# Sixteen sign pairs, swapped-part products and a new instruction order in a two-headed sequence kernel

## The chip, the cores and the metric

The kernel runs on one core of one Trainium2 chip. The metric is the device time of one execution in microseconds (us). Three runs of the kernel before gave 344.28, 345.22 and 346.68 us; their median is 345.22 us. One more execution was taken with the hardware profiler; its trace is the source of every duration below.

## The reference

Two independent results are computed for a sequence of 2048 positions and 448 channels, and joined along the channels.

```python
def _A_ref(x, wqkv, w_phi, wo):              # linear attention, 16 heads of 28
    q, k, v = (x @ wqkv), split into heads
    phi_q = concat(softmax(q @ w_phi), softmax(-(q @ w_phi)))     # phi_k likewise
    kv = einsum("bhsf,bhsd->bhfd", phi_k, v);  z = sum of phi_k over s
    o = (phi_q @ kv) / (phi_q . z + 1e-6)
    return o @ wo
def _B_ref(u, A, B, C, log_dt, Dskip):       # state-space convolution, 256 states a channel
    l = arange(2048) in bfloat16
    K = einsum("dn,dnl,dn->dl", C, exp(dt * A * l), dt * B).real
    return causal convolution of u with K (by FFT of length 4096) + u * Dskip
```

Because `l` is rounded to bfloat16, K has only 641 different positions.

## The kernel before

**The attention half.** A preparation folds `w_phi` into the key and query weights and transposes x. `key_side` then walks over 16 blocks of 128 positions: TensorE makes the key and value products (L577), ScalarE takes the exponentials with both signs (L580) and copies the values (L582), VectorE sums, inverts and scales (L584, L588, L590), TensorE accumulates (L594). `query_side` runs four times, on 512 positions each (q0 to q3): TensorE makes the query products (L610), ScalarE takes 8 exponentials (L613), TensorE makes the denominators (L619), VectorE divides (L626 to L631) and scales (L641), TensorE transposes and projects (L648, L654) and ScalarE copies (L650, L656).

**The convolution half.** The channels are worked through in four quarters `qt`, each in two chunks `c` of 112 columns. For every quarter there are two tables of complex powers. `U` has 16 high rows and is built by `hi_tables` on VectorE, doubling the rows with the powers 32, 64, 128 and 256 (`table_cmul`, L521 to L524, four operations for each product). `W` has 48 low rows at the positions `LO`: 15 pairs +p and -p, the rows 0 and 16 by themselves, and 16 far rows at 512, 1024 and 1536 plus something. `rotations(qt)` fills `T` with sines and cosines on ScalarE (L485, L486); `dampings(qt)` writes exponentials into `W` on ScalarE (L499, L502) and a negated copy (L503). Then `damp(qt, c)` on VectorE multiplies `W` by `T` (L535 on 15 rows of one part, L537 on one row) and makes the far rows from near ones with the conjugate of the power 512 (three `table_cmul`). `build_k` contracts both tables over the states on TensorE (L564) and ScalarE copies the result (L568). `scatter_k` moves it by DMA into `Kt`. `kernel_spectrum` (L697, copies L700), the spectrum of u (`signal_spectrum`, sums and differences at L305 and L306, products L317, copies L320) and `conv_group` (products L713, sums L718 to L760, `inverse` L725 to L729, TensorE L738) make the convolution in a transformed domain; the results are copied at L745 and stored.

**What sets the order.** `in_order` reads a table `ORDER` with one entry each for TensorE (PE), ScalarE (ACT), VectorE (DVE) and the DMA queue of SyncE (SP), and ties every engine to the order that it lists. No instruction can overtake another on its engine. The preparation, the key side, the four query parts and the four quarters are interleaved in this order. Most tables live in one large SBUF tile at byte offsets written in the code, so that buffers share space (for instance the ring `LATE` of late constants, `EQ` of the query exponentials, and the key weights `WpK` and `WV`).

ScalarE holds one set of function tables at a time; an `ACT_TABLE_LOAD` row stands wherever the order goes from exponentials to sines or back. Copies and casts stand between both without a load.

Of the kernel before, what the change touches and what calls it, by code (L numbers as in the profile page):

```python
# [36 lines left out]
LO = [s * p for p in LO_ABS[:-1] for s in (1, -1)] + [0, 16]  # L37
# [57 lines left out]
def pair_rows(x2, row, t, col):  # L95
# [11 lines left out]
        '8{^3b6Y5Jf$Tog2C_YVvp0dKPh9Q4@xt{w8^JtU(*2MZ52W>;7_d`){S@B+R9&}>lv1dU0dK5ovINDB67xgl9iN6qtG(uIee=B9)ok3m'
        'grrhuGFx$M%8cN}G^?%OE?~|Xhp7OiMdG9Fh{ZdLlHgvfkjbOIVzXJD=`yq~-t+1c_hrB}W5cDjhjLWVr?-Q`zaNpp>)Ez!Ad|%Vnh0R'
        'M|7p4upn0NM;KV7>#=%?+NZ}B6r(=o(+&Bv^>;JqGzen*m*-+_0H@JT4r!Z&rsalB3b9{B%rIZG%)U+4yx+n+-CZ=ctkr0;#G@cC_q_O'
        'w&3e;~1aC*yD36Uy-~8J|^7;+v^w+z*p)g^cxh8P^F<VgI@!=l8(A#gy?V&3Ij~&i(zN&-NGF^NGALONLtJdXhdeOux@f)tybC;|Bd_b'  # L110
        '0>k#pAzi12r~VIS>bBqS$ClNfA25%^%e5ngxO~&tQYUcbes0W$?B`A{MRPy*YX(dNTU8Jq1-R2`$G=',
# [8 lines left out]
    "DVE":  # L120
        'c-mc)&uh~`5XIm3M-p41Jy@kE*eY1ilUORoA{IQ@qloCigCbu2j}$}@5$ZwkARdHD{e_BGK@`y<sHg`?8`~t$&+aB^BFpUe?VFu>Gm}l'
        'OOu6i~N7Ql!yy+6#4fl<6)?ee;nEp7Oe&TC+2k5s8?(gJ&Ro`LkAD(3Y<&^o1p4vXE2cY|KbHu#z(P+V6=rQa9_?hQp?v<#q#y-lojy?'
        'Br6_Ky&h3jCWzwA>)<$45vTBSN3*In>A-SdU$3F{WjCH5=$OWp7_HGSQ^u8!!f(|#3SU{a=s5nsk`MsyNxr5kk-yA9r}uaVh|`#!Yx5I'
        'fnQSm<tp-j}^d?I)N+sbh3m!siMTNd4QhdJnr_pIpW&x2C>p0B@}txtsCsHc*4ULsZ^Z&Aa!ehN7N0%wt|J-Ql-N5r_4G(~Lec&kohj='
        '$%9MX?^yTzIdIOYRp_<?QUGAUge8J3U~0G*AlNGD5Y+zT8~O=pq3Z(+H+K3Pv`*JEz}R8p7VCH|2hcYCU2?1+YGwFDqY>+UyaNdnRBKe'
        'UhS%<VN$JwbLeFa_Y3R|6$N|{uGUwpG1Foo{|Ku=g#~qo8EiOBz5wO%4Q|)psFr5grk7#=X!K_)<Nqq4%8>sba3d!=',
# [65 lines left out]
def kernel(  # L192
# [214 lines left out]
    for i, k in enumerate((256, 512)):  # L407
        act(s2[:, :, :], cur[:, :, :], ACT.Square)
        nxt = qa[(i + 1) % 2]
        TT(out=nxt[:, 0, :], in0=s2[:, 0, :], in1=s2[:, 1, :], op=ALU.subtract)  # L410
# [81 lines left out]
    def dampings(qt):
        for c in range(2):
            p = args(AT, slice((2 * qt + c) * COLS, (2 * qt + c + 1) * COLS), 4)
            for e, n, f, rows_ in evals(4):
                last = rows_.start == N_ABS - 1
                for sgn in (1,) if last else (-1, 1):
                    a = 2 * rows_.start + (sgn < 0)
                    act(W[:, c, a + last:a + last + 2 * (rows_.stop - 1 - rows_.start) + 1:2 * rows_.step, 0, :], p[:, e:e + n],  # L499
                        ACT.Exp, scale=float(sgn * f))  # L500
# [2 lines left out]
            act(W[:, c, 1:30:2, 1, :], W[:, c, 1:30:2, 0, :], ACT.Copy, scale=-1.0)  # L503
# [25 lines left out]
    def damp(qt, c):  # L529
        xs = slice(c * COLS, (c + 1) * COLS)  # L530
        w = W[:, c]
        for sgn in (-1, 1):
            r = w_rows(0, N_ABS - 1, sgn)
            for cs_ in (1, 0):
                yield TT(out=w[:, r, cs_, :], in0=w[:, r, cs_ if sgn < 0 else 0, :], in1=T[:, cs_, 0:N_ABS - 1, xs], op=ALU.mult)  # L535
        for cs_ in (1, 0):
            yield TT(out=w[:, 31, cs_, :], in0=w[:, 31, cs_, :], in1=T[:, cs_, N_ABS - 1, xs], op=ALU.mult)  # L537
# [339 lines left out]
```

## Time and profile before

| | |
|---|---|
| median of three runs | 345.22 us |
| profiled execution | 347.15 us |
| its span (first to last instruction) | 345.4 us |
| mean granted TensorE clock | 0.883 |
| PE busy | 252.9 us (73%) in 3735 instructions |
| DVE busy | 295.9 us (86%) in 447 instructions |
| ACT busy | 237.5 us (69%) in 534 instructions |
| POOL busy | 16.1 us (5%) in 30 instructions |

The table is a mean over stages that have different limits. The stages have to be read apart: the preparation to 46.46 us, where ScalarE's first table load for the key side starts; the key side with q0's exponentials to about 120.9; the stretch of q1 and q2 to 176.9, where q2's last exponential ends; the other quarters and the convolution to 334.9, where VectorE ends; and 10.5 us in which the last products, copies and stores follow.

### The profile page before, as it was taken

The numbers are of one execution on the slowest core, as the hardware profiler recorded it, in microseconds if no ns is written. First come the engines' busy times: TensorE is split into PE (matmuls) and PEld (weight loads), VectorE is DVE, ScalarE is ACT, GpSimd is POOL, SyncE is SP. The second block draws the span as 40 slices with busy tenths as digits, with TensorE's granted clock in tenths as the row PEclk, the third lists the DMA queues.
The fourth block names the chain that finished last, engine by engine and source line by source line (L and its number), as shares of the span: only waits on it lengthen the run. The fifth ranks groups of instructions, "written<-read, shape, count | busy, mean of one in ns | idle before, by whom it ended". The sixth has DMA issues, their size and how long they took to land.

```text
span 345.4 us, 8960 instructions
## 1 busy us (share of the span) xinstructions
PE 252.9 (73%) x3735; PEld 184.4 (53%) x3735; DVE 295.9 (86%) x447; ACT 237.5 (69%) x534; POOL 16.1 (5%) x30
## 2 busy tenths in 40 slices
PE   0394595986898657999898768596657874399974
PEld 0372354444454434565587447365636764399874
DVE  3598999799989998842989999999799999999970
ACT  4689979899997828857849799897874413025401
POOL 3001000000000000000000000001000006300000
PEclk9998567699999958999999998569688999699968
DMA  6982020001123321121210020238522197750006
GB/s 179 264 241 60 22 68 19 0 36 45 54 68 107 102 73 53 70 69 68 72 51 17 29 69 3 47 74 243 195 59 66 38 380 243 125 110 2 2 2 213
DMA packets 30985, 31.43 MB, mean 91 GB/s; under 512 B 9329, under 2 KB 29633, under 8 KB 30561
## 3 DMA queue, kind: packets, MB, share of 16 engines
q1 hardware_dynamic: 28856, 25.42, 25.0%
q0 software_dynamic: 1616, 5.22, 5.6%
q8 instruction: 29, 0.48, 0.6%
q10 hardware_dynamic: 472, 0.23, 0.2%
q14 instruction: 12, 0.09, 0.1%
HBM read 22.94 MB, written 7.34 MB: 88 GB/s over the span
## 4 chain that ended last, share of the span: by engine, by line
PE 27%; DVE 23%; ACT 14%; issue 5%; DMA 2%; SPq 0%; DVEq 0%; ACTq 0%
ACT sbuf L499 5%; PE bank_65 L564 4%; DVE sbuf L535 3%; DVE sbuf L713 3%; PE bank_72 L697 3%; PE bank_66 L564 3%; DMA sbuf<-in_B_u_dram 2%; DVE sbuf L641 2%; PE bank_65 L738 2%; PE bank_72 L317 2%; PE bank_66 L738 2%; DVE sbuf L756 2%; ACT sbuf L700 1%; DVE sbuf L521 1%; ACT sbuf L613 1%
## 5 line engine op out<-in xcount | busy, mean ns | idle before, releaser
L564 PEld LDWEIGHTS <-sbuf 128*16 128x16 bf16 x1792 | 37.3, 115 | 15.8 <-issue 14.7
L317 PE MATMUL bank_72<-sbuf 128*128 128x448 bf16 x128 | 31.0, 365 | 7.7 <-ACT sbuf L320 7.6
L738 PEld LDWEIGHTS <-sbuf 128*128 128x128 bf16 x384 | 29.7, 107 | 12.0 <-issue 11.4
L522 DVE TENSOR_TENSOR sbuf<-sbuf 128x896 bf16<-128x896 bf16 (+2 forms) x44 | 35.6, 811 | 0.6
L521 DVE TENSOR_TENSOR sbuf<-sbuf 128x896 bf16<-128x896 bf16 (+2 forms) x44 | 35.5, 809 | 0.6
L535 DVE TENSOR_TENSOR sbuf<-sbuf 128x1680 bf16<-128x1680 bf16 x32 | 32.3, 1026 | 3.0 <-ACT sbuf L503 1.9
L697 PE MATMUL bank_72<-sbuf 128*128 128x112 bf16 (+1 forms) x256 | 25.0, 244 | 9.5 <-ACT sbuf L700 9.0
L697 PEld LDWEIGHTS <-sbuf 128*128 128x128 bf16 x336 | 22.8, 100 | 15.0 <-issue 13.5
L564 PE MATMUL bank_66<-sbuf 128*16 128x48 bf16 x896 | 23.4, 263 | 6.7 <-issue 5.2
L700 ACT CAST sbuf<-bank_72 128x448 bf16<-128x448 f32 x28 | 15.3, 546 | 15.1 <-PE bank_72 L697 15.1
L564 PE MATMUL bank_65<-sbuf 128*16 128x48 bf16 x896 | 23.8, 262 | 2.4 <-DVE sbuf L523 1.3
L713 DVE TENSOR_TENSOR sbuf<-sbuf 128x3584 bf16<-128x3584 bf16 (+1 forms) x9 | 23.6, 2645 | 0.6 <-ACT sbuf L700 0.4
L320 ACT CAST sbuf<-bank_72 128x448 bf16<-128x448 f32 x32 | 19.2, 599 | 5.5 <-PE bank_72 L317 5.5
L317 PEld LDWEIGHTS <-sbuf 128*128 128x128 bf16 x128 | 12.3, 100 | 18.8 <-issue 11.0
L577 PEld LDWEIGHTS <-sbuf 112*128 112x128 bf16 x128 | 13.2, 106 | 15.9 <-issue 8.6
L523 DVE TENSOR_TENSOR sbuf<-sbuf 128x448 bf16<-128x448 bf16 (+2 forms) x44 | 21.2, 483 | 0.5
L524 DVE TENSOR_TENSOR sbuf<-sbuf 128x448 bf16<-128x448 bf16 (+2 forms) x44 | 21.0, 479 | 0.6
L499 ACT ACTIVATE sbuf<-bank_68 128x112 bf16<-128x112 f32 (+2 forms) x60 | 18.2, 456 | 4.7 <-PE bank_65 L564 4.7
L584 DVE TENSOR_REDUCE sbuf<-sbuf 128x32 f32<-128x896 bf16 x16 | 17.3, 1080 | 2.2 <-ACT sbuf L580 2.2
L499 ACT ACTIVATE sbuf<-bank_67 128x112 bf16<-128x112 f32 (+2 forms) x60 | 18.4, 448 | 0.0
L577 PE MATMUL bank_70<-sbuf 112*128 112x448 bf16 x64 | 16.2, 379 | 2.2 <-ACT sbuf L582 2.1
L638 PEld LDWEIGHTS <-sbuf 112*128 112x128 bf16 x128 | 9.4, 104 | 14.9 <-issue 13.4
(177 smaller groups left out, 613.2 us busy)
## 6 DMA issues: line engine op xcount, KB each, us to landing
sbuf<-const SPq DMA_DIRECT2D x32, 224.0 KB
SUd<-sbuf SPq DMA_DIRECT2D x16, 224.0 KB
sbuf<-const SPq DMA_DIRECT2D x2, 1024.0 KB
sbuf<-in_A_x_dram SPq DMA_DIRECT2D x4, 448.0 KB
out_dram<-sbuf SPq DMA_DIRECT2D x16, 112.0 KB
sbuf<-SUd POOLq DMA_DIRECT2D x1, 1792.0 KB, 12.4
sbuf<-in_B_u_dram SPq DMA_DIRECT2D x4, 448.0 KB
sbuf<-SUd POOLq DMA_DIRECT2D x2, 896.0 KB, 10.0
```

What stands on the lines that cost most here:

```text
L317: mm(p[:, 0:D_MODEL].rearrange("p (q g x) -> p q g x", q=4, g=4), lhsT=G1[:, cp, jt, 128 * mt:128 * mt + 128], rhs=by_quarter(ab[:, cp ^ s ...
L499: act(W[:, c, a + last:a + last + 2 * (rows_.stop - 1 - rows_.start) + 1:2 * rows_.step, 0, :], p[:, e:e + n], ACT.Exp, scale=float(sgn * f))
L521: yield TT(out=flat[2], in0=flat[1], in1=pw(1), op=ALU.mult)
L522: yield TT(out=flat[0], in0=flat[1], in1=pw(0), op=ALU.mult)
L523: yield TT(out=d[0], in0=d[0], in1=t[1], op=ALU.add if conj else ALU.subtract)
L524: yield TT(out=d[1], in0=d[1], in1=t[0], op=ALU.subtract if conj else ALU.add)
L535: yield TT(out=w[:, r, cs_, :], in0=w[:, r, cs_ if sgn < 0 else 0, :], in1=T[:, cs_, 0:N_ABS - 1, xs], op=ALU.mult)
L564: mm(p[32 * g:32 * g + N_HI, qq * N_LO:(qq + 1) * N_LO], lhsT=U[qt % 2][:, c, :, ri, xc], rhs=W[:, c, :, ri, xc], start=(i == 0), stop=(i ...
L577: mm(p[:, :], lhsT=xT[:, dj, ts], rhs=w[:, dj, :], start=(dj == 0), stop=(dj == 3))
L697: mm(p[:, k2, :].rearrange("p (q g x) -> p q g x", q=nq, g=4), lhsT=f_tiles[i][1][:, fi, :], rhs=natural(Kt[:, kt, :] if kt < 5 else K0[:, ...
L713: TT(out=T[:, i], in0=su.unsqueeze(1).to_broadcast([128, 2, 2, n8]), in1=sk.unsqueeze(2).to_broadcast([128, 2, 2, n8]), op=ALU.mult)
L738: mm(p[:, k2, :], lhsT=GI[r][:, cp, mt, 128 * jt:128 * jt + 128], rhs=S[:, r, cp, mt, :], start=(cp == 0 and mt == 0), stop=False)
```

## The change

`LO` swaps the positions 0 and 16, so that rows 30 and 31 are +16 and 0 and all 16 values of `T` serve one pair of rows. `dampings` writes the positive exponential into part 1 of the even rows and the negative one into part 0 of the odd rows, with one exponential fewer a chunk. `damp` multiplies the 15 odd rows in both parts in one operation (L534 after), and the 16 even rows in another that reads part 1 for both parts (L535 after). The far rows take three operations instead of four for each product: one product with `far` (the imaginary part of the power 512 and its negative) that reads the near rows with the parts swapped (`flipped`, a negative stride over the parts), one product with the real part, and one addition (L539, L540, L542 after). ScalarE makes the negative by a new Copy (L416 after). The last doubling in `hi_tables` takes both chunks at once, `signal_spectrum` takes two blocks at a time, and `inverse` makes two subtractions in one. Scratch space, `qa[0]`, `WpK` and `WV` move to other offsets. The tables of `ORDER` are new for all four engines.

Line numbers after the change are higher by one or two than before (L580 is L582, L582 is L584, L320 is L321, L485 and L486 are L487 and L488, L499 is L496, L503 is L498, L613 is L615, L626 is L628, L641 is L643, L590 is L592).

```diff
@@ -34,7 +34,7 @@
 ODD = list(range(1, 16, 2))
 LO_ABS = [1, 3, 5, 7, 9, 11, 13, 15, 2, 6, 10, 14, 4, 12, 8, 16]
 N_ABS = len(LO_ABS)
-LO = [s * p for p in LO_ABS[:-1] for s in (1, -1)] + [0, 16]
+LO = [s * p for p in LO_ABS[:-1] for s in (1, -1)] + [16, 0]
 LO += [512 + p for p in LO[24:32]]
 LO += [1024 + p for p in LO[28:32]]
 LO += [1536 + p for p in LO[28:32]]
@@ -99,35 +99,34 @@
 
 ORDER = {
...
     "ACT":
-        'c-nPSTW?HJ6#n*^8KtCSs#BMmkTT=asj9og0~HCco<%(P0e*@XFHM@X!832(@FJ0_AQVwFgeLSdM$@=WeZIBNc6z2s&&t~CTkEX7&bl2'
...
+        'c-nPS+e(!|6#i!anx`<NQi~3PT4I`8?MS4VBHak}6wwoiZ_q3B3eklZK|}|#D72_;Wk_j;S{FOQ3d!2G^Xr@S&+mb~Wie~keCsf4)>@M'
...
...
 }
 
 def in_order(tc):
@@ -233,6 +232,7 @@
     AT = sb("AT", [128, 2, NCOL], BF16, oAT)
     TH = sb("TH", [128, 2, NCOL], BF16, oTH)
     PW = {k: sb(f"PW{k}", [128, 2, NCOL], BF16, oPW + 3584 * i) for i, k in enumerate((32, 64, 128, 256, 512))}
+    far = sb("far", [128, 2, NCOL], BF16, oPW + 16128)
     PW[16] = sb("PW16", [128, 2, NCOL], BF16, oTs)
     ident = PID[:, 0, :]
     first = sb("first", [128, 128], BF16, oMISC + 256)
@@ -249,8 +249,8 @@
     Wqk = sb("Wqk", [112, 4, 2 * D_MODEL], BF16, oW)
     wT = sb("wT", [112, 2, 4, D_MODEL], BF16, oW + 7168)
     BD = sb("BD", [112, 4, 112], BF16, oW + 14336)
-    WpK = sb("WpK", [112, 4, D_MODEL], BF16, oPW + 17920)
-    WV = sb("WV", [112, 4, D_MODEL], BF16, oPW + 21504)
+    WpK = sb("WpK", [112, 4, D_MODEL], BF16, oEQ)
+    WV = sb("WV", [112, 4, D_MODEL], BF16, oEQ + 3584)
 
     ldt = sb("ldt", [4, 112], BF16, oMISC + 32)
     id4 = sb("id4", [4, 4], BF16, oMISC + 8)
@@ -297,13 +297,14 @@
 
     def signal_spectrum(b, copy):
         ab = sb("ab", [128, 2, 4, D_MODEL], BF16, oT + 14336)
-        for t in range(4):
-            ua = sb(f"ua{b}", [128, 2, D_MODEL], BF16, oON, bufs=4)
-            for a in range(2):
-                nc.sync.dma_start(out=ua[64 * a:64 * a + 64, 0, :], in_=rep_rows(u2, 1024 * b, a, t))
-            nc.sync.dma_start(out=ua[:, 1, :], in_=pair_rows(u2, 1024 * b, t, 0))
-            TT(out=ab[:, 0, t, :], in0=ua[:, 0, :], in1=ua[:, 1, :], op=ALU.add)
-            TT(out=ab[:, 1, t, :], in0=ua[:, 0, :], in1=ua[:, 1, :], op=ALU.subtract)
+        for t in range(0, 4, 2):
+            ua = sb(f"ua{b}", [128, 2, 2, D_MODEL], BF16, oON, bufs=2)
+            for t2 in range(2):
+                for a in range(2):
+                    nc.sync.dma_start(out=ua[64 * a:64 * a + 64, 0, t2, :], in_=rep_rows(u2, 1024 * b, a, t + t2))
+                nc.sync.dma_start(out=ua[:, 1, t2, :], in_=pair_rows(u2, 1024 * b, t + t2, 0))
+            TT(out=ab[:, 0, t:t + 2, :], in0=ua[:, 0], in1=ua[:, 1], op=ALU.add)
+            TT(out=ab[:, 1, t:t + 2, :], in0=ua[:, 0], in1=ua[:, 1], op=ALU.subtract)
         i = 0
         for st in range(2):
             for cp in range(2):
@@ -367,7 +368,7 @@
 
     LOWP = (128, 16, 32, 64)
     amp = {k: sb(f"amp{k}", [128, NCOL], F32, oU + 3584 * i) for i, k in enumerate(LOWP)}
-    qa = [sb(f"qa{i}", [128, 2, NCOL], F32, (oEQ, oT + 8192)[i]) for i in range(2)]
+    qa = [sb(f"qa{i}", [128, 2, NCOL], F32, (oPW + 17920, oT + 8192)[i]) for i in range(2)]
     s2 = sb("s2", [128, 2, NCOL], F32, oW + 36736)
 
     def cmul(dst, src, pw, tmp):
@@ -412,6 +413,7 @@
                                        op0=ALU.mult, op1=ALU.mult)
         nc.scalar.copy(PW[k][:, :, :], nxt[:, :, :])
         cur = nxt
+    act(far[:, 1, :], cur[:, 1, :], ACT.Copy, scale=-1.0)
     p = psum("st", [128, D_MODEL])
     for nch in range(2):
         mm(p.rearrange("p (g c q) -> p c g q", g=4, c=NCHK), lhsT=first[:, :],
@@ -485,21 +487,14 @@
             act(T[:, 0, rows_, :], p[:, e:e + n], ACT.Sin, scale=float(f), bias=bias_hp[:, :])
             act(T[:, 1, rows_, :], p[:, e:e + n], ACT.Sin, scale=float(f))
 
-    def w_rows(j0, n, sgn):
-        a = 2 * j0 + (sgn < 0) if j0 < N_ABS - 1 else 2 * j0 + 1 + (sgn < 0)
-        return slice(a, a + 2 * n - 1, 2)
-
     def dampings(qt):
         for c in range(2):
             p = args(AT, slice((2 * qt + c) * COLS, (2 * qt + c + 1) * COLS), 4)
             for e, n, f, rows_ in evals(4):
-                last = rows_.start == N_ABS - 1
-                for sgn in (1,) if last else (-1, 1):
-                    a = 2 * rows_.start + (sgn < 0)
-                    act(W[:, c, a + last:a + last + 2 * (rows_.stop - 1 - rows_.start) + 1:2 * rows_.step, 0, :], p[:, e:e + n],
-                        ACT.Exp, scale=float(sgn * f))
-                if last:
-                    act(W[:, c, 31, 1, :], p[:, e], ACT.Exp, scale=float(f))
+                for neg in (1, 0) if rows_.start < N_ABS - 1 else (0,):
+                    a = 2 * rows_.start + neg
+                    act(W[:, c, a:a + 2 * (rows_.stop - 1 - rows_.start) + 1:2 * rows_.step, 1 - neg, :], p[:, e:e + n],
+                        ACT.Exp, scale=float(f - 2 * f * neg))
             act(W[:, c, 1:30:2, 1, :], W[:, c, 1:30:2, 0, :], ACT.Copy, scale=-1.0)
 
     def spread(qt, k, c, n):
@@ -509,6 +504,12 @@
             return lambda i: PW[k][:, i, cols].rearrange("p (c x) -> p c x", c=2).unsqueeze(2).to_broadcast([128, 2, n, COLS])
         cols = slice((2 * qt + c) * COLS, (2 * qt + c + 1) * COLS)
         return lambda i: PW[k][:, i, cols].unsqueeze(1).to_broadcast([128, n, COLS])
+
+    def flipped(v):
+
+        ap = [list(d) for d in v.ap]
+        ap[2][0] = -ap[2][0]
+        return bass.AP(tensor=v.tensor, offset=v[:, :, 1, :].offset, ap=ap)
 
     def table_cmul(dst, src, pw, tmp, conj=False):
 
@@ -529,20 +530,21 @@
     def damp(qt, c):
         xs = slice(c * COLS, (c + 1) * COLS)
         w = W[:, c]
-        for sgn in (-1, 1):
-            r = w_rows(0, N_ABS - 1, sgn)
-            for cs_ in (1, 0):
-                yield TT(out=w[:, r, cs_, :], in0=w[:, r, cs_ if sgn < 0 else 0, :], in1=T[:, cs_, 0:N_ABS - 1, xs], op=ALU.mult)
-        for cs_ in (1, 0):
-            yield TT(out=w[:, 31, cs_, :], in0=w[:, 31, cs_, :], in1=T[:, cs_, N_ABS - 1, xs], op=ALU.mult)
+        t = T[:, :, :, xs].rearrange("p i n x -> p n i x")
+        yield TT(out=w[:, 1:30:2], in0=w[:, 1:30:2], in1=t[:, 0:N_ABS - 1], op=ALU.mult)
+        yield TT(out=w[:, 0:31:2], in0=w[:, 0:31:2, 1, :].unsqueeze(2).to_broadcast([128, N_ABS, 2, COLS]), in1=t, op=ALU.mult)
+        cols = slice((2 * qt + c) * COLS, (2 * qt + c + 1) * COLS)
         for d0, s0, n in ((32, 24, 8), (40, 36, 4), (44, 40, 4)):
-            yield from table_cmul(w[:, d0:d0 + n], w[:, s0:s0 + n], spread(qt, 512, c, 2 * n),
-                                  scratch(oT2 + 3584, n, c), conj=True)
+            src, dst, t2 = w[:, s0:s0 + n], w[:, d0:d0 + n], scratch(oPW + 19712, n, c)
+            yield TT(out=t2, in0=flipped(src), in1=far[:, :, cols].unsqueeze(1).to_broadcast([128, n, 2, COLS]), op=ALU.mult)
+            yield TT(out=dst, in0=src, in1=PW[512][:, 0, cols].unsqueeze(1).unsqueeze(1).to_broadcast([128, n, 2, COLS]),
+                     op=ALU.mult)
+            yield TT(out=dst, in0=dst, in1=t2, op=ALU.add)
 
     def hi_tables(qt):
         u = U[qt % 2]
         yield nc.vector.tensor_copy(u[:, :, 0], CB[:, :, qt * QC:(qt + 1) * QC].rearrange("p i (c x) -> p c i x", c=2))
-        for k, n, chunks in ((32, 1, (None,)), (64, 2, (None,)), (128, 4, (None,)), (256, 8, (0, 1))):
+        for k, n, chunks in ((32, 1, (None,)), (64, 2, (None,)), (128, 4, (None,)), (256, 8, (None,))):
             for c in chunks:
                 src, dst = ((u[:, :, h:h + n] if c is None else u[:, c, h:h + n]) for h in (0, n))
                 yield from table_cmul(dst, src, spread(qt, k, c, 2 * n), scratch(oT2, n, c))
@@ -723,8 +725,9 @@
             S = sb(f"S{b}{gi}", [128, 2, 2, 4, cols], BF16, oCB + 14336 + 4 * n8 * b)
             y = Y[:, b]
             TT(out=S[:, 0].rearrange("p c m x -> p c (m x)"), in0=y[:, :, 0], in1=y[:, :, 1], op=ALU.add)
-            TT(out=S[:, 1, 0].rearrange("p m x -> p (m x)"), in0=y[:, 0, 0], in1=y[:, 0, 1], op=ALU.subtract)
-            TT(out=S[:, 1, 1].rearrange("p m x -> p (m x)"), in0=y[:, 1, 1], in1=y[:, 1, 0], op=ALU.subtract)
+            up, down = (bass.AP(tensor=y.tensor, offset=y[:, 0, st].offset, ap=[list(y.ap[0]), [2 * n4 + n4 - 2 * st * n4, 2], [1, n4]])
+                        for st in range(2))
+            TT(out=S[:, 1].rearrange("p c m x -> p c (m x)"), in0=up, in1=down, op=ALU.subtract)
             if gi == 0:
                 TT(out=UD[:, b], in0=UD[:, b], in1=DSK[:, :].unsqueeze(1).unsqueeze(1).to_broadcast(
                     [128, 2, 4, D_MODEL]), op=ALU.mult)
@@ -787,8 +790,8 @@
         tc.cur_priority = old
 
     for c in range(2):
-        nc.gpsimd.memset(W[:, c, 30, 0, :], 1.0)
-        nc.gpsimd.memset(W[:, c, 30, 1, :], 0.0)
+        nc.gpsimd.memset(W[:, c, 31, 0, :], 1.0)
+        nc.gpsimd.memset(W[:, c, 31, 1, :], 0.0)
     rotations(0)
     with rank(9000):
         key_side()
```

**ScalarE in the first half of the key side.** L580 and L582 (L582 and L584 after) are the key side's exponentials and copies, L485 and L486 (L487 and L488) the sines of the first quarter, L320 (L321) a copy of the spectrum of u. Before:

```order
L499 ACTIVATE sbuf<-bank_68 128x112
L502 ACTIVATE sbuf<-bank_68 128x112
L486 ACT_TABLE_LOAD
L486 ACTIVATE sbuf<-bank_67 128x2x224
L320 CAST sbuf<-bank_72 128x448
L485 ACTIVATE sbuf<-bank_67,sbuf 128x224
L486 ACTIVATE sbuf<-bank_67 128x224
L582 CAST sbuf<-bank_70 128x448
L485 ACTIVATE sbuf<-bank_67,sbuf 128x224
L320 CAST sbuf<-bank_72 128x448
L486 ACTIVATE sbuf<-bank_67 128x224
L485 ACTIVATE sbuf<-bank_67,sbuf 128x224
```

After:

```order
L488 ACT_TABLE_LOAD
L488 ACTIVATE sbuf<-bank_67 128x224
L321 CAST sbuf<-bank_72 128x448
L487 ACTIVATE sbuf<-bank_67,sbuf 128x224
L584 CAST sbuf<-bank_70 128x448
L582 ACT_TABLE_LOAD
L582 ACTIVATE sbuf<-bank_69 128x448 x2
L321 CAST sbuf<-bank_72 128x448
L582 ACTIVATE sbuf<-bank_71 128x448 x2
L584 CAST sbuf<-bank_70 128x448
L488 ACT_TABLE_LOAD
L488 ACTIVATE sbuf<-bank_67 128x224
```

The sines of the first quarter stood in runs of up to a dozen behind one load; now they stand in ones and twos between the key exponentials, with a load on either side. The exponentials of `dampings(0)` (L499, L502) have left the key side. Of the 17 loads of the whole program before, 2 stand ahead of the key side, 9 in it with q0's exponentials, 2 from there to q2's last exponential and 4 behind. After the change these are 2, 19, 4 and 4, so 29.

**ScalarE behind q0's exponentials.** The first row shows where `dampings(0)` has gone (L496, copy L498); L652 and L658 are q0's copies, L414 the cast of the power 512 that stood in the preparation before, L416 is new. After:

```order
L496 ACT_TABLE_LOAD
L496 ACTIVATE sbuf<-bank_68 128x4x112 x4
L496 ACTIVATE sbuf<-bank_68 128x2x112 x4
L496 ACTIVATE sbuf<-bank_68 128x112 x3
L652 CAST sbuf<-bank_70 112x512
L496 ACTIVATE sbuf<-bank_68 128x112 x4
L321 CAST sbuf<-bank_72 128x448
L496 ACTIVATE sbuf<-bank_67 128x4x112
L658 CAST sbuf<-bank_71 128x448
L496 ACTIVATE sbuf<-bank_67 128x4x112 x2
L321 CAST sbuf<-bank_72 128x448
L496 ACTIVATE sbuf<-bank_67 128x4x112
```

In the order before, this place had the sines of the second quarter (L485, L486) behind q0's exponentials. They now follow behind both chunks of `dampings(0)`.

**VectorE where the `damp` of the third quarter begins.** L535 and L537 before are the multiplications of `W` by `T`, L521 to L524 the far rows, L641 (L643 after) the scaling of a query part. Before:

```order
L522 TENSOR_TENSOR sbuf<-sbuf 128x2x448
L535 TENSOR_TENSOR sbuf<-sbuf 128x15x112
L537 TENSOR_TENSOR sbuf<-sbuf 128x112 x2
L535 TENSOR_TENSOR sbuf<-sbuf 128x15x112 x3
L641 TENSOR_TENSOR sbuf<-bank_70,sbuf 128x448
L522 TENSOR_TENSOR sbuf<-sbuf 128x1792
L641 TENSOR_TENSOR sbuf<-bank_71,sbuf 128x448
L521 TENSOR_TENSOR sbuf<-sbuf 128x1792
L521 TENSOR_TENSOR sbuf<-sbuf 128x896
L535 TENSOR_TENSOR sbuf<-sbuf 128x15x112
L641 TENSOR_TENSOR sbuf<-bank_71,sbuf 128x448
L535 TENSOR_TENSOR sbuf<-sbuf 128x15x112 x3
```

After:

```order
L535 TENSOR_TENSOR sbuf<-sbuf 128x16x224
L643 TENSOR_TENSOR sbuf<-bank_69,sbuf 128x448
L534 TENSOR_TENSOR sbuf<-sbuf 128x15x224
L643 TENSOR_TENSOR sbuf<-bank_70,sbuf 128x448
L540 TENSOR_TENSOR sbuf<-sbuf 128x1792
L539 TENSOR_TENSOR sbuf<-sbuf 128x1792
L643 TENSOR_TENSOR sbuf<-bank_70,sbuf 128x448
L535 TENSOR_TENSOR sbuf<-sbuf 128x16x224
L643 TENSOR_TENSOR sbuf<-bank_71,sbuf 128x448
L534 TENSOR_TENSOR sbuf<-sbuf 128x15x224
L643 TENSOR_TENSOR sbuf<-bank_71,sbuf 128x448
L540 TENSOR_TENSOR sbuf<-sbuf 128x1792
```

Two operations of 15 or 16 rows by 224 stand for four of 15 rows by 112 and two single rows; L540 and L539 are the two products of the far rows, and L542 is their sum.

On SP the four loads of u for the skip product (L836, L839 after) followed directly on the last scatter of the third quarter; they now stand behind seven more loads of constants (L684 after), in two pairs with four more between them.

More of the change, by code (lines that the diff above doesn't have):

```diff
@@ L107 @@
[L107 to L111, printed above, removed]
@@ L120 @@
-    "DVE":
[L121 to L126, printed above, removed]
+        'c-q}qF=!hx6umoRiic1<++a!u4;?&Y$PkJL4<>|CN`_EOF(rd3o=S#NOzDu(Lx)g2WC$fghEPH=A%qU0c*xKpLx&6<Jb1|9p%haxcnH|'
@@ new lines @@
+    "DVE":
+        'c-mD`*-8UJ5UkzV#MLJwY(S&YN0ESr5U(Hbi~Rw?2d|(34+QbSgLnmlAc?^(YbIl|%QDkPbys&!ZvkY=04b-X{Ynd9kl>w(v^SQemGR<'
+        'as0b?q;V~Yi5BbSC^jJby@nlaH*>#MGd;$7g63-qYygKdxhm4#YvWO-uXNV(@*{|X5(~PIC7=u>EQ^RG(TGhGX#42i<(K%s5otCig&`s'
+        'G^?g%?}+P1H}g)@&Fcz?>7F~99`Ab*T=))m>5-R6cmYT!cCq&oICdbv^Mm0a$<@MYLL#3G)=RPm^Bxnb@L^ll^0JWGcQ=x|=U2vK(X`J'
+        'j!T#TV@xK5z}U{GU8T<hiZf%`siEhBnu6t>_w_Sy67)akn^y>^ucT-ZpMecg*v~V?9w{wsIBU9PQLrvwaM_Z4hR92*=X6O0n`x28r>L;'
+        'pu0#G2tlqf7j%YKN?Tq`T',
@@ L131 @@
+        '<DlfR49T5_EFT{Cqp_B46)>eQ4mOa8n$|J(MIs#TWR3BSJIfWeGn',
 }
```

31 lines of the change are left out of this document (17 added, 14 removed).

## The prediction

> **The bound.** I read the stages first, because the page's shares are means over all of them. The columns are the length of a stretch, busy time of PE, PE's weight loads, DVE, ACT and POOL with their instruction counts, the clock, the DMA share and GB/s.
>
> ```profile
> 0.00:46.46 46.46, 22.99 (x186) 16.56 (x187) 34.73 (x47) 36.31 (x65) 4.73 (x16) 0.85 0.55 146
> 46.46:120.90 74.44, 59.74 (x387) 33.99 (x385) 68.92 (x117) 69.02 (x147) 0.00 (x0) 0.91 0.17 56
> 120.90:176.90 56.00, 47.43 (x620) 29.51 (x620) 40.67 (x77) 39.15 (x92) 0.00 (x0) 0.91 0.20 68
> 176.90:334.90 158.00, 117.25 (x2452) 99.01 (x2450) 151.59 (x209) 90.85 (x227) 11.36 (x14) 0.87 0.34 94
> 334.90:345.40 10.50, 5.53 (x100) 5.37 (x97) 0.00 (x0) 2.13 (x4) 0.00 (x0) 0.83 0.52 176
> ```
>
> Three different kernels stand here. In the key side DVE (68.9 of 74.4 us) and ACT (69.0) are both nearly full. In the stretch of q1 and q2 nothing is full: DVE has 15.3 us idle, ACT 16.9. Behind it DVE is the bound, with 151.6 busy of 158.0, and everything ends 10.5 us after it. So an instruction taken from DVE is worth its time behind 176.9, and little between 120.9 and 176.9 unless DVE's waits there go too. Next the waits of both engines in the early part, with their total, number and longest:
>
> ```profile
> ACT sbuf L650 <- PE bank_70 L648: 7.9, 2, 6.7
> ACT sbuf L320 <- PE bank_72 L317: 5.5, 5, 2.2
> ...
> DVE sbuf L626 <- PE bank_70 L619: 5.7, 1, 5.7
> DVE sbuf L641 <- PE bank_70 L638: 3.4, 2, 2.9
> DVE sbuf L641 <- PE bank_71 L638: 2.4, 1, 2.4
> ```
>
> DVE stands at q1's reciprocal (L626) until TensorE has the denominators, which need ACT's exponentials (L613). ACT stands at q0's copies (L650) until DVE's scaled rows have gone through TensorE. The attention chain crosses from engine to engine, and whoever is late in it delays the rest. The crossing at which the bound changes hands is q2:
>
> ```profile
> 175.81 1.09 ACT L613 ACTIVATE sbuf<-bank_69 112x512 bf16<-112x512 f32 x2
> 181.61 0.98 ACT L499 ACTIVATE sbuf<-bank_68 128x448 bf16<-128x448 f32 x2 [4.71 <-PE bank_65 L564]
> ...
> 178.19 0.96 DVE L626 RECIPROCAL sbuf<-bank_70 128x128 f32<-128x128 f32 x1 [0.99 <-PE bank_70 L619]
> ```
>
> ACT's last exponential of q2 ends at 176.9, and DVE takes up the denominators 1.3 us later, after a wait of 0.99. From here DVE hardly stops. I therefore cut the sum at this point: how much later or earlier ACT reaches the end of q2's exponentials, and how much shorter DVE's part behind it is.
>
> **DVE.** The change takes away 86 instructions of 447. It keeps every element that is multiplied and joins operations, so only the fixed part of an operation goes. The rows of three sizes:
>
> ```profile
> L535 DVE TENSOR_TENSOR sbuf<-sbuf 128x1680 bf16<-128x1680 bf16 x32 | 32.3, 1026 | 3.0 <-ACT sbuf L503 1.9 <-ACT sbuf L499 0.7 <-ACT sbuf L486 0.2
> L522 DVE TENSOR_TENSOR sbuf<-sbuf 128x1792 bf16<-128x1792 bf16 x20 | 21.6, 1085 | 0.2
> L524 DVE TENSOR_TENSOR sbuf<-sbuf 128x896 bf16<-128x896 bf16 x20 | 12.2, 614 | 0.2
> L537 DVE TENSOR_TENSOR sbuf<-sbuf 128x112 bf16<-128x112 bf16 x16 | 2.9, 210 | 0.0
> L713 DVE TENSOR_TENSOR sbuf<-sbuf 128x7168 bf16<-128x7168 bf16 x3 | 11.7, 3891 | 0.1
> ```
>
> From 1792 to 7168 elements it is (3891 - 1085) / 5376 = 0.522 ns an element, which leaves 150 ns fixed. But not all of that is paid between two operations:
>
> ```profile
> 217.18 2.91 DVE L535 TENSOR_TENSOR sbuf<-sbuf 128x1680 bf16<-128x1680 bf16 x3
> ...
> 236.23 1.09 DVE L521 TENSOR_TENSOR sbuf<-sbuf 128x1792 bf16<-128x1792 bf16 x1
> 237.36 0.62 DVE L524 TENSOR_TENSOR sbuf<-sbuf 128x896 bf16<-128x896 bf16 x1
> ```
>
> Three independent operations of 1026 ns take 2.91 us, so they start (2910 - 1026) / 2 = 942 ns apart; 0.522 x 1680 is 877, and the paid fixed part is about 67 ns. A successor that needs the result starts at 237.36, 1.13 behind 236.23, where 67 + 0.522 x 1792 = 1002 would do; a dependent step costs some 0.12 more. I take 67 ns an operation removed, and 0.12 where a dependent step goes.
>
> One `damp` before, at 67 ns and 0.522 an element: four of 1680 (3.77 us) and two of 112 (0.25) are 4.02. After: one of 3360 and one of 3584 are 1.82 + 1.94 = 3.76, so 0.27 less. The far rows lose three operations, 0.20. Together 0.47, eight times: 3.8 us. The joined doubling by 256 loses four operations (0.27) and one dependent step (0.12), 0.39, four times: 1.6. `signal_spectrum` loses eight, 0.5; `inverse` six, 0.4. In all 6.3 us; at the whole 150 ns it would be 86 x 0.15 = 12.9, which is the upper bound. Behind q2 lie five of the eight chunks, two of the four doublings and `inverse`: 2.35 + 0.78 + 0.4 = 3.5 us, which I round to 3.6 with the fragment of high rows that the new order puts ahead of q2. The other 2.7 us lie ahead of it, where DVE has 15.3 us to spare, and I count them as nothing. Without that cover they would be worth 2.7.
>
> The Trainium skill ("VectorE: DVE Perf Modes", The DRAIN you can't avoid) says that the next operation does not start until the pipe is empty, by which each removed one would be worth the whole fixed part. The row of three L535 above speaks against it: 2.91 us for three of 1.026.
>
> **ACT.** The new order has twelve table loads more. Rows of the place where the order goes from sines to exponentials, and the group's line:
>
> ```profile
> L486 ACT ACT_TABLE_LOAD x4 | 5.1, 1283 | 0.1
> 92.41 0.44 ACT L486 ACTIVATE sbuf<-bank_67 128x224 bf16<-128x224 f32 x1
> 92.87 1.28 ACT L580 ACT_TABLE_LOAD   x1
> 94.16 0.54 ACT L580 ACTIVATE sbuf<-bank_71 128x448 bf16<-128x448 f32 x1
> ```
>
> From the sine's start to the exponential's it is 1.75 us. Without a load one operation overlaps the next by some 0.14 us (below, three of 0.57 take 1.44 and so start 0.43 apart), so a load costs 1.75 - 0.30 = 1.45, its 1.28 and the overlap that it breaks; I take 1.5. Ahead of q2's end the loads go from 13 to 25, +18.0 us; behind it four stay four.
>
> The dampings of the first quarter go from the key side to behind q0's exponentials:
>
> ```profile
> 95.45 1.44 ACT L499 ACTIVATE sbuf<-bank_67 128x448 bf16<-128x448 f32 x3
> 185.69 1.24 ACT L499 ACTIVATE sbuf<-bank_68 128x224 bf16<-128x224 f32 x6
> 186.97 1.60 ACT L503 ACTIVATE sbuf<-sbuf 128x1680 bf16<-128x1680 bf16 x1
> ```
>
> The largest start (1.44 - 0.57) / 2 = 0.43 apart. The smaller ones, with a last one of 0.44, start (1.24 - 0.44) / 5 = 0.16 apart in this row, which mixes two sizes; I take 0.2. A chunk is then 4 x 0.43 + 11 x 0.2 and a copy of 1.5, some 5.4 us; two chunks are 10.8. So the key side with q0 gets ten loads (+15.0), loses the dampings (-10.8) and four small operations (-1.6): +2.6. The stretch of q1 and q2 gets two loads (+3.0), the dampings (+10.8), the cast of the power 512 (+1.6), the new Copy (+0.85) and some sines that come later (+1.1): +17.3. The preparation loses the cast and a wait of 1.05 us on L417, whose copy moves behind the first key exponentials: I take -2.2.
>
> ACT's programme is then 46.46 - 2.2 = 44.3 us to the key side, 69.0 + 2.6 = 71.6 in it, and 39.2 + 17.3 = 56.5 to the end of q2's exponentials, 172.4 in all, against 176.9 now. To this comes what ACT still waits. Before, it waited 5.4 + 16.9 = 22.3 us in the two stretches. Call the new waiting i: the point is reached at 172.4 + i, and the span changes by (172.4 + i - 176.9) - 3.6 = i - 8.1. The bounds of i are 0 and the 22.3 of now. I take 6: the key side's 5.4 are short waits for TensorE that more load in between does not lengthen, and in the query stretch ACT is now full (56.5 us of work against 56.0), so the others run ahead and have the data ready when it asks. That is a choice, and the widest uncertainty of the forecast.
>
> The span so changes by 6 - 8.1 = -2.1: 343.3 us in the terms of the profiled span, 345.0 of its own execution time of 347.15, and 343.1 against the median of 345.22, which was 1.9 below the profiled run.
>
> **The rest.** No wait is added on DVE by the new `damp` that the old one did not have; it needs all exponentials of a chunk instead of one sign, and behind q2 ACT has 67 us of idle time to be early in. SP's later loads of u could make L729 late:
>
> ```profile
> 275.33 7.79 DMA sbuf<-in_B_u_dram
> ...
> 283.11 0.03 issue
> ...
> 283.36 3.95 DVE sbuf L729 x2
> ```
>
> They landed 0.2 us before their use; the new order has one more 3.9 us product ahead of that use, and seven ring loads of about 1 us ahead of the issue. I take 0, between a loss of 3 and a gain of 1.
>
> **Rivals.** (1) *The loads land on the path*, the slower side: ACT's sines in ones and twos stand between exponentials for which DVE and TensorE wait, so that filling a wait in one place opens one in another. If i stays at three quarters of now, 16, the span grows by 7.9, to 353.1. It turns slower than before from i = 8.1. For it speaks that ACT becomes the bound from 44 to 180; against it, that ACT already ran 93% full in the key side. (2) *ACT hardly waits* and the order fits as a whole: i = 1 gives -7.1, 338.1. For it speaks that dampings and `damp` of the first quarter now lie where both engines had 15 to 17 us idle. (3) *Reads with the parts swapped run at half speed*, as the f32 rows do:
>
> ```profile
> L410 DVE TENSOR_TENSOR sbuf<-sbuf 128x896 f32<-128x896 f32 x2 | 2.2, 1090 | 0.0
> ```
>
> Then L539 costs 0.522 x 3584 = 1.9 us more a chunk, 9.3 for the five behind q2: 352.4. No row before reads with a negative step; the innermost step stays one, which speaks against it. (4) *Fewer operations save nothing*, because DVE's gaps there belong to waits on ACT and TensorE: 345.2 with the new waits just covered by the earlier start. (5) *A switch holds ACT for twice its row*, once to empty and once to load: twelve times another 1.28 us would give 343.1 + 15.4 = 358.5. The load above, with a neighbour that ends at 92.85 and one that starts at 94.16, leaves no room for that.
>
> The Trainium skill ("ScalarE: Activation LUTs", What ACT_TABLE_LOAD costs) gives 1283 ns and a drain of about 1380, 2.66 us a switch, and asks for calls batched by set, which the new order does not do; rival 5 is the row's nearest form of it. The 1283 agree with the trace, the drain does not appear in it.
>
> **Chances.** The forecast (i from 3 to 9, so 340 to 346) has 0.45, of which 0.14 lie more than 1% below the median; 1% is about what a measurement can tell from no change (341.8 to 348.7). Rival 1 has 0.22, rival 2 0.23, rival 3 0.04, rival 4 0.05, rival 5 0.01. Faster is 0.14 + 0.23 = 0.37, the same 0.31 + 0.05 = 0.36, slower 0.27. The range goes to 336.5 (i = 0 with a little of the uncounted 2.7) and up to 351, which leaves out most of rivals 1, 3 and 5, some 0.2.
>
> **Signs.** DVE with some 361 instructions and about 290 us of summed time; L534 near 1.9 us and L535 near 2.0; L539 equal to L540. ACT with 29 loads of 1.28 us, and in the stretches of key and queries over 92% busy. q2's last exponential near 178.4 and the last DVE operation near 332.7. The forecast is wrong if q2's exponentials end beyond 182 or before 175, or if DVE's waits behind q2 grow from the 6.4 us that it has there now.

## The result, and the profile after

The changed kernel takes 336.67 us (median of four, 334.94 to 337.87) against 345.95 us of the kernel before in the same runs: a ratio of 0.973, interval 0.967 to 0.980. A second set gave 337.68 us and 0.974 (0.970 to 0.978). So it is 9 us faster, 2.6 to 2.7%; the forecast was 343.1, and the second rival's 338.1 came nearest. The profiled span went from 345.4 to 335.6 us, 9.8 less. Executions that took over 1.5% longer than the fastest of their kernel are left out of the medians and ratios below, but the profile of the kernel with the new operations in the old order is of such a one (379.57 us).

The stages of the kernel after, with the columns of the first view of the prediction. The key side now ends with q0's last exponential at 114.3, which was 118.96 before; the two rows behind the dots are the kernel before, cut there.

```profile
0.00:45.70 45.70, 24.18 (x191) 17.38 (x192) 31.41 (x44) 34.77 (x65) 4.74 (x16) 0.84 0.57 152
45.70:114.30 68.60, 54.69 (x362) 31.12 (x360) 63.76 (x97) 67.50 (x118) 0.00 (x0) 0.96 0.15 49
114.30:173.60 59.30, 52.18 (x792) 33.20 (x793) 46.21 (x62) 57.52 (x135) 0.00 (x0) 0.94 0.20 63
...
46.46:118.96 72.50, 58.80 (x375) 33.28 (x373) 66.98 (x113) 67.11 (x145) 0.00 (x0) 0.91 0.17 54
118.96:176.90 57.94, 48.37 (x632) 30.22 (x632) 42.62 (x82) 41.06 (x94) 0.00 (x0) 0.91 0.21 69
```

ACT (the fourth busy time) is full in both stretches, 67.5 of 68.6 and 57.5 of 59.3 us. Its waiting there fell from 22.3 to 2.9 us, while its work grew by 16.9. The waits say the same: DVE hardly waits at a reciprocal any more (0.2 us in all), and ACT's long wait at q0's copies is gone.

```profile
ACT sbuf L652 <- PE bank_69 L650: 1.1, 1, 1.1
ACT sbuf L321 <- PE bank_72 L318: 0.6, 1, 0.6
...
DVE sbuf L534 <- ACT sbuf L498: 5.4, 3, 2.7
DVE sbuf L643 <- PE bank_69 L640: 2.9, 1, 2.9
DVE sbuf L628 <- PE bank_70 L621: 0.2, 1, 0.2
```

Now the three points at which I cut the span: q2's last exponentials, q2's reciprocal, VectorE's last operation.

```profile
172.51 1.09 ACT L615 ACTIVATE sbuf<-bank_71 112x512 bf16<-112x512 f32 x2
...
176.00 0.95 DVE L628 RECIPROCAL sbuf<-bank_70 128x128 f32<-128x128 f32 x1
...
327.11 0.62 DVE L730 TENSOR_TENSOR sbuf<-sbuf 128x896 bf16<-128x896 bf16 x1
```

The reciprocal starts 2.2 us earlier than before (178.19). From there DVE needs 151.7 us to its end at 327.73, where it needed 156.7: 5.0 less. Behind it stand 7.9 us instead of 10.5: 2.65 less. These three make the 9.8 us.

### The profile page after: what moved, and what is told of

It is laid out like the page before. It is cut to its first block, busy times and chain, and to the rows that moved or that the text cites. A ratio compares the mean times of both kernels' runs of the same rounds, so it can differ in the third digit from the quotient of the medians.

```text
span 335.6 us, 8869 instructions
## 1 busy us (share of the span) xinstructions
PE 255.6 (76%) x3735; PEld 182.7 (54%) x3735; DVE 289.3 (86%) x361; ACT 252.2 (75%) x539; POOL 16.1 (5%) x30
## 5 line engine op out<-in xcount | busy, mean ns | idle before, releaser
L699 PE MATMUL bank_72<-sbuf 128*128 128x112 bf16 (+1 forms) x256 | 29.9, 271 | 10.5 <-ACT sbuf L702 9.6
L539 DVE TENSOR_TENSOR sbuf<-sbuf 128x896 bf16<-128x896 bf16 (+1 forms) x24 | 18.6, 776 | 2.0 <-ACT sbuf L416 1.8
L579 PE MATMUL bank_70<-sbuf 112*128 112x448 bf16 x64 | 15.3, 362 | 6.2 <-ACT sbuf L584 6.2
L534 DVE TENSOR_TENSOR sbuf<-sbuf 128x3360 bf16<-128x3360 bf16 x8 | 15.2, 1903 | 5.4 <-ACT sbuf L498 5.4
L321 ACT CAST sbuf<-bank_72 128x448 bf16<-128x448 f32 x32 | 18.9, 591 | 0.6 <-PE bank_72 L318 0.6
L542 DVE TENSOR_TENSOR sbuf<-sbuf 128x896 bf16<-128x896 bf16 (+1 forms) x24 | 18.7, 779 | 0.6
L496 ACT ACTIVATE sbuf<-bank_67 128x112 bf16<-128x112 f32 (+2 forms) x60 | 19.2, 470 | 0.0
L540 DVE TENSOR_TENSOR sbuf<-sbuf 128x896 bf16<-128x896 bf16 (+1 forms) x24 | 18.6, 776 | 0.4
L535 DVE TENSOR_TENSOR sbuf<-sbuf 128x3584 bf16<-128x3584 bf16 x8 | 16.1, 2018 | 2.9 <-ACT sbuf L496 2.9
L640 PEld LDWEIGHTS <-sbuf 112*128 112x128 bf16 x128 | 9.3, 105 | 14.4 <-issue 9.3
L496 ACT ACTIVATE sbuf<-bank_68 128x112 bf16<-128x112 f32 (+2 forms) x60 | 17.0, 448 | 0.0
```

Source lines behind the costliest of these rows:

```text
L321: copy(sg[:, k2, :], p[:, 0:D_MODEL])
L496: act(W[:, c, a:a + 2 * (rows_.stop - 1 - rows_.start) + 1:2 * rows_.step, 1 - neg, :], p[:, e:e + n], ACT.Exp, scale=float(f - 2 * f * neg))
L539: yield TT(out=t2, in0=flipped(src), in1=far[:, :, cols].unsqueeze(1).to_broadcast([128, n, 2, COLS]), op=ALU.mult)
L540: yield TT(out=dst, in0=src, in1=PW[512][:, 0, cols].unsqueeze(1).unsqueeze(1).to_broadcast([128, n, 2, COLS]), op=ALU.mult)
L542: yield TT(out=dst, in0=dst, in1=t2, op=ALU.add)
L579: mm(p[:, :], lhsT=xT[:, dj, ts], rhs=w[:, dj, :], start=(dj == 0), stop=(dj == 3))
```

## The experiments

**The old operations in the new order.** All 86 operations are back at the places of those that replaced them; ScalarE, TensorE and the DMA queue are as in the changed kernel.

```diff
-        yield TT(out=w[:, 1:30:2], in0=w[:, 1:30:2], in1=t[:, 0:N_ABS - 1], op=ALU.mult)
+        for cs_ in (1, 0):
+            yield TT(out=w[:, 1:30:2, cs_, :], in0=w[:, 1:30:2, cs_, :], in1=t[:, 0:N_ABS - 1, cs_, :], op=ALU.mult)
...
-        for k, n, chunks in ((32, 1, (None,)), (64, 2, (None,)), (128, 4, (None,)), (256, 8, (None,))):
+        for k, n, chunks in ((32, 1, (None,)), (64, 2, (None,)), (128, 4, (None,)), (256, 8, (0, 1))):
```

> The changed kernel with all 86 VectorE operations put back at the places of those that replaced them; ScalarE, TensorE and the DMA queue keep the new order with its 29 table loads. Theory A (the operations give their start-to-start price behind q2 and the order gives the rest): 3.5 to 5 us more than the changed kernel, 340 to 342 us, with VectorE's part behind q2's reciprocal back from 151.7 us towards 156.7 and q2's reciprocal still near 176. Theory B (the whole gain is the order's): 336 to 338. Theory C (the whole gain is the operations'): 344 to 347.

Measured: 341.65 us, ratio to the kernel before 0.988 (0.985 to 0.991). Theory A, except that q2's reciprocal came at 177.5 and not near 176. The operations are worth 5.0 us (the two intervals, 0.967 to 0.980 and 0.985 to 0.991, do not overlap), and what is left of the change, called the order here, 4.2; besides the order it holds the new places of buffers and ScalarE's changed operations. DVE's stretches, up to q2's reciprocal and from there to its end (its busy time is the third), for this kernel and, behind the dots, for the changed one:

```profile
0.00:177.50 177.50, 134.90 (x1419) 84.70 (x1423) 146.78 (x244) 162.75 (x325) 4.73 (x16) 0.91 0.27 80
177.50:332.04 154.54, 121.38 (x2269) 98.08 (x2261) 149.45 (x205) 88.19 (x214) 11.37 (x14) 0.82 0.38 102
332.04:339.80 7.76, 3.14 (x64) 2.98 (x61) 0.00 (x0) 1.06 (x2) 0.00 (x0) 0.83 0.59 200
...
0.00:176.00 176.00, 133.42 (x1411) 83.83 (x1415) 143.67 (x207) 162.19 (x321) 4.74 (x16) 0.92 0.28 81
176.00:327.73 151.73, 119.00 (x2270) 95.81 (x2266) 145.65 (x156) 88.92 (x217) 11.38 (x14) 0.85 0.38 103
327.73:335.60 7.87, 3.21 (x66) 3.05 (x63) 0.00 (x0) 1.06 (x2) 0.00 (x0) 0.93 0.60 203
```

Behind the reciprocal 49 operations fewer save 3.8 us of work, and the stretch is 2.8 us shorter. Ahead of it 37 fewer save 3.1 us of work, and the reciprocal comes 1.5 us earlier. The last stretch is 7.8 to 7.9 us with either set, so its shortening belongs to the order.

**The new operations in the old order.** The changed kernel's code with the places of before on TensorE, ScalarE and VectorE; the DMA queue keeps the new order.

```diff
 ORDER = {
-    "PE": the changed kernel's places
+    "PE": the places before; ACT and DVE likewise, SP as changed
```

> The changed kernel's operations in the order of before on TensorE, ScalarE and VectorE, so with 17 table loads and with the first quarter's dampings in the key side again; a joined operation stands where the last of its parts stood (the joined doubling where its first chunk stood). The DMA queue keeps the new order, since the new buffers ask for it. Theory A: 3.5 us less than before, 341 to 343. Theory B (order alone): 344 to 347, as before. Theory C (operations alone): 336 to 338.

Measured: 374.24 us (median of three), 1.083 (1.079 to 1.086), which none of the theories allowed. The profiled span is 377.8 us, 32.4 more than before. Of these, 5.5 us have come by the end of the preparation (52.0 against 46.46), 9.8 by q2's reciprocal (187.95 against 178.19), and 22.6 more behind it. Three long waits:

```profile
ACT sbuf L361 <- DMA sbuf<-in_B_B_re_dram: 6.0, 1, 6.0
ACT sbuf L486 <- DVE sbuf L533: 11.4, 1, 11.4
DVE sbuf L731 <- DMA sbuf<-in_B_u_dram: 16.0, 2, 14.8
```

The first, in the preparation, and the third, behind q2, are waits for loads. I put them down to the DMA queue's order, which does not fit the other engines' old ones; no run separates that. The second is the join itself: the sines of the next quarter overwrite `T`. In the kernel before the first of them ran at 120.28, ahead of the last product with `T` at 126.97, which still needed only the other part of `T`; a joined product reads both parts and releases both at its end. If the 5.5 us of the preparation carry over whole, 4.3 of the 9.8 us at q2's reciprocal are left for this wait. So this run says nothing on the price of the operations, and the two halves of the change cannot be added up in both orders; it does show that a joined operation holds its inputs longer, and that the new operations do not fit the old order.

**Fewer, and more, table loads.** Only ScalarE's first-quarter sines move, here from ten runs into four. A cut of the order on ScalarE:

```diff
-L488 ACT_TABLE_LOAD
-L488 ACTIVATE sbuf<-bank_67 128x224
 L321 CAST sbuf<-bank_72 128x448
-L487 ACTIVATE sbuf<-bank_67,sbuf 128x224
 L584 CAST sbuf<-bank_70 128x448
-L582 ACT_TABLE_LOAD
 L582 ACTIVATE sbuf<-bank_69 128x448 x2
```

> The changed kernel with nothing but the first quarter's sines moved on ScalarE: they stand in four runs instead of ten, so 17 table loads instead of 29, some 18 us of ScalarE's time less ahead of q2. Theory A (ScalarE bounds the time up to q2, where it is over 97% busy): the key side shrinks until VectorE's 64 us of work bound it, 4 to 5 us less, near 332. Theory B (the loads fill time in which ScalarE would wait for the other engines): within 1% of the changed kernel, 334 to 340. Theory C (long runs of sines hold up the key exponentials): 2 to 5 us more, 339 to 342.

Measured: 335.20 us, 0.969 (0.963 to 0.974), against 0.973 of the changed kernel: 1.5 us, and the intervals overlap. That is theory B. Twelve loads fewer took 14.4 us of work from ScalarE and gave almost nothing back. The key side and the stretch of q1 and q2, DVE and ACT by their third and fourth busy times:

```profile
45.20:112.00 66.80, 55.30 (x385) 32.11 (x384) 63.33 (x97) 56.16 (x110) 0.00 (x0) 0.93 0.16 53
112.00:171.00 59.00, 51.28 (x786) 32.87 (x783) 46.63 (x62) 55.11 (x130) 0.00 (x0) 0.94 0.20 63
```

In the key side ACT has 10.6 us idle, DVE 3.5; in the second stretch ACT has 3.9. With 17 loads DVE is the fuller engine in the key side, with 29 ACT has caught up with it. The other direction, with six more sines put between exponentials:

> The changed kernel with the sines of the first quarter scattered further: 41 table loads instead of 29, 18 us more on ScalarE in the key side and behind it, nothing else changed. Theory A (ScalarE is the bound up to q2): 14 to 18 us more, 351 to 355. Theory B (loads are hidden): within 1%, 334 to 340. Half of it (344 to 348) would mean that the other engines still leave ScalarE idle time to be filled.

Measured: 354.31 us, 1.024 (1.020 to 1.028). That is 17.6 us for twelve loads, 1.47 each, as theory A has it. The key side of this kernel:

```profile
44.50:128.00 83.50, 60.64 (x357) 33.76 (x356) 64.41 (x98) 81.75 (x126) 0.00 (x0) 0.86 0.12 40
```

Three of the six:

> The changed kernel with three of the six additional scatterings of e_scatter: 35 table loads. Theory A (29 loads stand where ScalarE's spare time ends, each further one costs its whole 1.47 us): 6 x 1.47 = 8.8 more, 344 to 347. Theory B (some of the further loads still find idle time, so that the cost begins later): 338 to 342.

Measured: 346.56 us, 1.000 (0.996 to 1.004): theory A. The changed kernel ran in the same set, as the measure for it:

> The changed kernel itself once more, as the measure for the runs beside it: 335 to 338 us, VectorE's end 7.5 to 8 us ahead of the end of the span.

Measured: 337.68 us, 0.974, with VectorE's end 7.8 us ahead of the end of the span. Six loads cost 8.9 us, 1.48 each. So 17 and 29 loads take nearly the same time, and from 29 on each one is paid in full: six more eat the whole change.

**ScalarE's work moved forward.** On top of the four runs of sines, the first chunk of the first quarter's dampings, the cast of the power 512 and the negated Copy go into the key side.

```diff
 L582 ACTIVATE sbuf<-bank_71 128x448
+L496 ACTIVATE sbuf<-bank_68 128x4x112 x2
 L582 ACTIVATE sbuf<-bank_71 128x448
```

> The changed kernel with the sines gathered as in e_gather (17 table loads) and besides, on ScalarE alone, the first chunk of the first quarter's dampings, the cast of the power 512 and its negated Copy moved from the stretch of q1 and q2 forward into the key side, where e_gather left ScalarE 10.6 us idle. Theory A (up to q2 ScalarE's load is what counts, stretch by stretch): the stretch of the queries loses some 7.8 us of ScalarE's work and VectorE's waits for it there (6.1 us in e_gather), so 3 to 6 us less than the changed kernel, 330 to 334. Theory B (with 17 loads the other engines bound both stretches, ScalarE no longer): as e_gather, 333 to 337.

Measured: 335.78 us, 0.971 (0.966 to 0.976): theory B. Of the 6.1 us of VectorE's waits that I had meant to remove, 1.0 was left, and others came or grew in their place:

```profile
DVE sbuf L641 <- PE bank L638: 6.1, 4, 2.9
DVE sbuf L641 <- ACT sbuf L319: 3.8, 1, 3.8
...
ACT sbuf L650 <- PE bank L648: 6.4, 1, 6.4
```

This and the kernel with 17 loads are the fastest that were run; neither is shown to beat the changed kernel.

**The last stretch.** TensorE's last products in the kernel before, with the wait ahead of them in brackets; then two groups of eight some us later, and behind the dots one of the changed kernel's and one of the new operations in the old order:

```profile
330.56 0.91 PE L738 MATMUL bank_65<-sbuf 128*128 128x112 bf16 x8 [3.23 <-DVE sbuf L725]
333.68 0.95 PE L738 MATMUL bank_66<-sbuf 128*128 128x112 bf16 x8
336.29 0.56 PE L738 MATMUL bank_65<-sbuf 128*128 128x112 bf16 x8
...
327.24 0.55 PE L741 MATMUL bank_67<-sbuf 128*128 128x112 bf16 x8 [1.77 <-DVE sbuf L727]
362.92 0.91 PE L740 MATMUL bank<-sbuf 128*128 128x112 bf16 x8 [3.23 <-DVE sbuf L726]
```

After a wait of 3.23 us eight products take 0.91 to 0.95 us for some five us, then 0.56; the granted clock from 330 to 334 us is 0.50. After a wait of 1.77 us they take 0.55 at once. With the new operations in the old order the wait of 3.23 us is there again, the slow products behind it too, and the last stretch is 10.8 us. To test this, idle products fill the wait in the kernel before:

```diff
+    for _ in range(60):
+        mm(psum.banks[7][:, 0:112], lhsT=ident, rhs=G1[:, 0, 0, 0:112], start=True, stop=True)
     in_order(tc)
```

> The kernel before with 60 idle products of 128x112 into an unused bank, placed on TensorE just where it waited 3.2 us for VectorE ahead of its last 144 products; nothing else changed. Theory A (the shorter end of the changed kernel comes from TensorE's clock, which the wait had halved): the last products run at full clock, the stretch behind VectorE's end goes from 10.5 to about 8 us, 2 to 2.6 us less than before, 342 to 344. Theory B (it comes from the order of the sums and products): the end stays at 10.5 us or grows, 344.5 to 347.

Measured: 346.29 us, 0.9995 (0.996 to 1.003): no difference in the times, as theory B has it. Its profiled execution shows what theory A asked for:

```profile
330.79 0.55 PE L738 MATMUL bank<-sbuf 128*128 128x112 bf16 x8 [0.16 <-DVE sbuf L725]
...
335.12:343.30 8.18, 3.23 (x66) 3.07 (x63) 0.00 (x0) 1.06 (x2) 0.00 (x0) 0.98 0.65 221
```

The products run at full clock, the last stretch is 8.2 us instead of 10.5 and the span 343.3. So in the profiled executions the clock makes 2.3 of the 2.65 us; in the times a gain of that size from it is not found, and why stays open. Part of it is which executions were profiled: over all of this set the median span is 344.7 us for the kernel before and 344.25 with the idle products, so the profiled 345.4 lies above its median and the profiled 343.3 below.

## Why the prediction was right or wrong

The time fell inside the range, but at its very end (336.67, where the range began at 336.5), and by its own sign the forecast was wrong: q2's exponentials ended at 173.6 us, and an end before 175 was named as such a sign. In spans, 343.3 was forecast and 335.6 came. Of the 7.7 us between them, 3.7 had come by q2's reciprocal, 1.4 came behind it and 2.65 in the last stretch. The low end of the range stood for i = 0 and a little of VectorE's uncounted work. The last stretch was not in it, so that the range held is in part luck. The terms one by one:

- **DVE's 6.3 us of work.** Right. DVE's busy time fell from 295.9 to 289.3 us, by 6.6, and by 6.9 between the two sets of operations in one order. Per operation removed that is 80 ns of work and, by the times, 5.0 / 86 = 58 ns of the run, against 67 in the sum; the whole fixed part of 150 ns would have been 12.9 us. Rival 4, by which fewer operations save nothing, is ruled out by the same 5.0 us. The wait for an empty pipe that the Trainium skill describes ("VectorE: DVE Perf Modes", The DRAIN you can't avoid) is not what these operations pay; the same section adds that a next operation that is not held starts earlier, as the prediction's row of three L535 shows.
- **3.6 us behind q2, nothing ahead of it.** The first half held (the stretch 2.8 us shorter, 3.8 less work); the other 2.2 of the 5.0 us behind q2 are the order's. The second half did not hold: 1.5 us came ahead of q2. I had taken DVE's 15.3 us of idle time there as cover. In the new order DVE reaches q2's reciprocal with a wait of 0.2 us, so its own work counts there.
- **ACT's programme of 172.4 us to the end of q2's exponentials.** Close: 45.7 + 67.5 + 57.5 = 170.7. The two stretches got 16.9 us of work more, not 19.9, and the preparation lost 0.8, not 2.2. The price of a load was right: 1.47 and 1.48 us in the runs, 1.5 in the sum. They rule out rival 5. Rival 1, the loads on the path, did not come with 29 loads; each load beyond them does lie on it. The 2.66 us a switch of the Trainium skill ("ScalarE: Activation LUTs", What ACT_TABLE_LOAD costs) is not what these loads cost.
- **The waiting i = 6.** This is the term of the sum that was most mis-sized: 2.9 were left. Together with the smaller programme, ACT reached the point 3.3 us earlier than before where I had it 1.5 later. The argument was sound (a full engine finds its data ready), the number was not: I left the key side's 5.4 us whole, and they fell to 1.1. Rival 2 (i = 1) put the point at 173.4, and 173.6 came, by less work and a little more waiting than it had. Its reason, that dampings and `damp` lie where both engines were idle, fits the stages; no run tests it.
- **Its own bound.** I treated q2 as ACT's to set. ACT's 3.3 us became 2.2 at the reciprocal, because DVE came to it only then. The kernels with 17 loads agree: with ScalarE relieved by 14.4 us, the time hardly falls.
- **The last stretch at 0.** Missed by 2.65 us in the profile. I had looked at the loads of u there and not at TensorE's wait and its clock behind it. How much of this the times hold is open, as said above.
- **Negative steps, rival 3.** No cost: L539, which reads the parts swapped, and L540, which does not, take the same time.

```profile
L540 DVE TENSOR_TENSOR sbuf<-sbuf 128x1792 bf16<-128x1792 bf16 x8 | 8.7, 1085 | 0.1
L539 DVE TENSOR_TENSOR sbuf<-sbuf 128x1792 bf16<-128x1792 bf16 x8 | 8.7, 1087 | 1.9 <-ACT sbuf L416 1.8
L534 DVE TENSOR_TENSOR sbuf<-sbuf 128x3360 bf16<-128x3360 bf16 x8 | 15.2, 1903 | 5.4 <-ACT sbuf L498 5.4
L535 DVE TENSOR_TENSOR sbuf<-sbuf 128x3584 bf16<-128x3584 bf16 x8 | 16.1, 2018 | 2.9 <-ACT sbuf L496 2.9
```

What the order gives by itself, 4.2 us in the times, is by the profiled spans 5.6: 0.7 at q2's reciprocal, 2.2 behind it and 2.75 in the last stretch. The profiled execution of the kernel before was 1.2 us above its median, which is most of the difference. Of the 2.2 about 1.2 are four operations of high rows that the order puts ahead of q2. That the first quarter's dampings and `damp` moved into the idle stretch is what lets it carry twelve more loads is argued from the stages; the order was not taken apart further.

## What to carry to other kernels

An engine's idle time in a stage is a budget that a reordering can spend on costs which look bad by themselves: here twelve table loads, 14.4 us of work, took ScalarE's waiting up to q2 from 14.5 us to 2.9 for nearly nothing, and the six behind them cost 1.48 us each. When a sum depends on how much waiting is left, forecast it from which engine is full after the change; a full engine's short waits go as well. Joining operations saves what their starts lie apart beyond the elements (60 to 80 ns each here), and more of it where the engine bounds the stage (2.8 of 3.8 us behind q2, 1.5 of 3.1 ahead of it); but the joined operation holds its inputs longer, so the order has to be looked at with it.

## What the runs showed of the hardware

In two traces TensorE fell to about half its clock (0.50 granted) after waiting 3.23 us and came back some five us later; waits of 1.24 and 1.77 us left it at full clock, and so did 60 idle products in place of the long wait. The Trainium skill ("TensorE: Matmul & The Clock Gate", Part 1: The HAM clock gate) puts the idle time from which it happens at about 3.4 us; the trace agrees in kind: the wait is a little shorter by the modelled end of the last product, and 3.44 us from the start of that product to the next.
